# Dense blocks on chip for both halves of batch 0, a clock model with two levels, and weight loads on GpSimd's queue

## The chip, the cores and the metric

One core of a Trainium2 chip runs the whole program. The metric is the device time of one execution in microseconds; the time before is the median of three executions, 964.66 us. The engines are named TensorE (PE, with its weight loads as PEld), VectorE (DVE), ScalarE (ACT), GpSimd (POOL) and SyncE (SP), which issues DMAs.

## What is computed

The reference takes q, k and v of 4 batches, 8 heads, 576 positions and 64 dimensions. For each head it adds two attentions, then runs two feed-forward layers over the 2304 tokens (512 wide, 2048 inside):

```python
out_d = sm_attn(q_d, k_d, v_d)               # q, k, v averaged over groups of 4 positions
out_up = np.repeat(out_d, 4, axis=2)
mask = np.abs(pos[:, None] - pos[None, :]) < 4
attn = softmax(where(mask, scale * q @ k.T, -1e9))
x = (out_up + attn @ v)                      # -> [2304, 512]
x = prelu(x @ w_in1, alpha) @ w_out1
y = elu(x @ w_in2) @ w_out2
```

The weights come as 64-bit floats, so each must be converted on the chip.

## The kernel before, in words

The program is one function, `fused_kernel`, in which a planner writes out one order of instructions for all engines. Work is cut into generators ("threads": `th_...`), each with a priority; `_Clock` models when each engine, the SP queue and the DMA rings would be free, and `run_while`, `fill` and `tick` pick the next thread by priority among those whose inputs would be ready. Each engine then runs its instructions strictly in that written order. All instructions go through `_Engine.call` (line 231), so nearly every row of the profile has L231 and groups are told apart by tiles.

**Feed-forward.** Layer 1 has 8 token groups of 288 (two per batch: u = 0 and u = 1), each with 16 steps f of 128 inner columns. A step s multiplies x with `wi` (12 matmuls, tiles xh and xl, `mm_in`), applies the activation (`th_elem`: tiles n, r, gh, gl) and multiplies with `wo` (12 matmuls, `out1`). The list `segs` orders them: segment 0 is group 0 with f = 0 to 9, then group 1 with all 16, then the rest of group 0, then groups 2 to 7. Group 1 is u = 1 of batch 0; groups 2 and 3 are batch 1. Layer 2 has 6 groups of 384 tokens.

**Weights.** An item is one f of `w_in` or `w_out`, 512 KB of 64-bit words. `th_ldw` issues the loads (`load_w`: SP, tiles rawi and rawo), in the order of `items`. `th_conv` converts an item: ScalarE makes cp, VectorE does one instruction on cp and two into cw, ScalarE writes the high half of wi or wo and VectorE the low half (`raw_a` to `raw_d`). The raw item and the converted one share a slot. In layer 1 some slots hold attention tiles first (`early`), so `th_ldw` waits: items 8 to 15 for the local attention of u = 0 (`pav`), 16 to 19 for the sums of v, 24 to 31 for q and k. From the fifth item on (`PF = 4`) a load also waits until the item four before it has been converted that far. All these waits are on SP, whose queue runs in order: what is behind a waiting DMA waits too.

**Attention of batch 0.** `th_pair` and `th_da0` make the averaged attention (tiles sm, P, pt, od). The local attention of u = 0 is `th_dense`: blocks of 64 queries by 70 keys per pair of heads p = 0 to 3, with a mask added by a matmul (`d_mm`), maximum (`d_max`, tile Dmx), exponent (`d_exp`, tile dP), normalisation (`d_norm`, Dden), five transposes (`d_tp`, `d_ev`) and the product with v (`d_av`, tile vd), all on chip; then `p_add` makes x. When all four pairs are done, SP writes x to DRAM (xsp), to be read again for the third segment. The local attention of u = 1 goes another way: `th_S0` multiplies blocks of 72 by 78, evicts them (ss) and writes them to DRAM (scr); `th_soft0` reads only the band of 7 diagonals (tile s), takes the softmax and writes the band into a zeroed pscr; `th_p` reads dense blocks back (pp), transposes them (ppT), multiplies with vb and adds. Batch 1 does this for both halves; batches 2 and 3 use VectorE. Threads of u = 1 start after step 0 (`slot` 0).

**Clock and warm-up.** `_Clock.pe` books TensorE's columns by stretches of time and takes matmuls at full or half speed by what the stretch before held. In `run_while`, while step 0 is not ready and the planner sees TensorE idle, it inserts matmuls of a constant tile (warm) as long as `quiet()` holds: booked columns below `MORE * BUSY`.

Of the kernel before, what the change touches and what calls it, by code (L numbers as in the profile page):

```python
# [40 lines left out]
MORE = 1.0  # L41
# [12 lines left out]
NB = 2  # L54
# [3 lines left out]
class _Clock:  # L58
    TICK, BUSY = 10240 / 3, 2640.0
# [4 lines left out]
    MANY = {"ACT": 70.0, "DVE": 93.0, "SP": 50.0, "PE": 0.0}  # L64

    def __init__(self):
        self.cols = {}
        self.t = dict.fromkeys(("PE", "ACT", "DVE", "SP", "DMA"), 0.0)
# [11 lines left out]
    def pe(self, t, cost, share):  # L80
        k = int(t / self.TICK)
        while cost > 0.0:
            slow = 1.0 if self.cols.get(k - 1, 0.0) >= self.BUSY else 2.0
# [82 lines left out]
    def dma(self, out, in_):  # L166
# [21 lines left out]
class _Engine:  # L188
# [31 lines left out]
    def __getattr__(self, op):  # L220
        fn = getattr(self.eng, op)

        def call(*args, **kw):
            if op == "dma_start":
                self.clock.dma(kw["out"], kw["in_"])
# [10 lines left out]
def fused_kernel(ctx: ExitStack, tc: tile.TileContext, qk, vt, vl, ql, kl, vb, w_in1, w_out1, alpha,  # L236
# [3 lines left out]
    PE, ACT, DVE, SP = (_Engine(n, e, ck) for n, e in  # L240
                        (("PE", nc.tensor), ("ACT", nc.scalar), ("DVE", nc.vector), ("SP", nc.sync)))
# [12 lines left out]
    maskf = const.tile([128, 2, QK], F32, name="maskf")  # L254
    maskb = const.tile([128, 5, QK], BF16, name="maskb")
    identb = const.tile([128, 128], BF16, name="identb")
    warm = const.tile([128, 4], BF16, name="warm")

# [9 lines left out]
    scr0 = {(b, u): dram.tile([1, BLK * (RW + 1)], F32, name=f"scr{b}_{u}") for b in range(NB) for u in range(2) if b or u}  # L268
# [97 lines left out]
    def d_mm(p, bk):  # L366
        t = st["qk", 0, p]
        ps = bk[:, 0:5 * QK]
        mk = maskb.rearrange("p j k -> p (j k)")
# [9 lines left out]
    def d_max(p, bk):  # L379
        st["dP", p] = early(PT0 + p, [128, 5 * QK + 5 * 128], F32, f"dP_{p}")  # L380
        mx = Ap.tile([128, 5, 1], F32, tag="Dmx", name="Dmx", bufs=2)
        st["dmx", p] = mx
# [4 lines left out]
    def d_exp(p, bk):  # L387
        den = Ap.tile([128, 5, 1], F32, tag="Dden", name="Dden", bufs=2)
        st["dden", p] = den
        for j in range(5):  # L390
            c = slice(j * QK, (j + 1) * QK)
            ACT.activation(out=st["dP", p][:, c], in_=bk[:, c], func=AF.Exp, scale=float(D) ** -0.5,
                           bias=st["dmx", p][:, j], accum_out=den[:, j])

    def d_norm(p):
        den = st.pop(("dden", p))
        P = st["dP", p][:, 0:5 * QK].rearrange("p (j k) -> p j k", j=5)
# [4 lines left out]
    def d_tp(p, bks):  # L402
        for j in range(5):
            bk = bks[j // 4]
            PE.transpose(bk[0:QK, (j % 4) * 128:(j % 4 + 1) * 128], st["dP", p][:, j * QK:(j + 1) * QK], ident)

    def d_ev(p, bks):
        t = st["dP", p][0:QK, 5 * QK:]
# [3 lines left out]
    def d_av(p, bk):  # L412
        t, v = st.pop(("dP", p))[0:QK, 5 * QK:].rearrange("k (j c) -> k j c", j=5), st.pop(("vd", p))
# [447 lines left out]
    def th_S0(p, u):  # L861
        tag = "ss"
        yield "key", "ld0", p, u
        yield "tok", tag
        bks = yield "bank", 2
        s_mm(0, p, 4 * u, 4, bks)
        finish("smm", 0, p, u)
        yield ("ACT",)
        t = s_ev(4, bks, tag)
        release(bks)  # L870
        yield ("SP",)
        s_write0(0, p, u, t)
        put(tag)
        finish("S", 0, p, u)

# [11 lines left out]
    def th_dense(p):  # L887
        yield "key", "ld0", p, 0
        bks = yield "bank", 1
        d_mm(p, bks[0])  # L890
        finish("smm", 0, p, 0)
        finish("S", 0, p, 0)
        yield ("DVE",)
        d_max(p, bks[0])
        yield ("ACT",)
        d_exp(p, bks[0])
        release(bks)
        yield ("DVE",)
        d_norm(p)
        bks = yield "bank", 2  # L900
        d_tp(p, bks)
        yield ("ACT",)
        d_ev(p, bks)
        release(bks)
        yield "key", "od1", 0, p, (0,)
        bks = yield "bank", 1
        d_av(p, bks[0])
        finish("pav", 0, p, 0)
        yield ("DVE",)
        p_add(0, p, 0, bks[0])  # L910
        release(bks)
        x = st["x", 0, 0].rearrange("p k t j -> p k (t j)")
        yield ("ACT",)
        ACT.activation(out=xs["h"][:, p], in_=x[:, p], func=AF.Copy)
        yield ("DVE",)
        DVE.tensor_tensor(out=xs["l"][:, p], in0=x[:, p], in1=xs["h"][:, p].bitcast(F32), op=ALU.subtract)
        tm["x"] = max(tm["x"], ck.cur["t"])
        finish("xcp", p)
        finish("pa", 0, p, 0)
        if all(("pa", 0, z, 0) in done for z in range(NP)):  # L920
            finish("xa", 0, 0)
            SP.dma_start(out=xsp, in_=st.pop(("x", 0, 0)).rearrange("p k t j -> p k (t j)"))
# [132 lines left out]
    def th_soft0(b, u):  # L1055
        for p in range(NP):
            yield "key", "S", b, p, u
        if b and u:
            for p in range(NP):
                yield "key", "pr", b - 1, p, u  # L1060
# [39 lines left out]
    def th_vb(b, u):  # L1100
        if b:
            yield "key", "vb", b - 1 + u, 1 - u
# [123 lines left out]
    def th_ldw(ly):  # L1226
        for k, it in enumerate(items):
            if ly == 2:
                yield "key", "fr", (2,) + it
            else:  # L1230
# [4 lines left out]
                elif V0 <= k < SH0:  # L1235
                    yield "key", "sv", 0, k - V0
# [4 lines left out]
                if k >= PF:  # L1241
                    yield "key", "cv", 1, k - PF
# [189 lines left out]
    with tc.manual_schedule():  # L1432
# [3 lines left out]
        for p in range(NP):  # L1436
# [9 lines left out]
            if p:  # L1446
                at(0.0)
                load_vd(p - 1)
        at(0.0)
        load_vd(NP - 1)  # L1450
        at(0.0)
        ACT.activation(out=maskb[:, 0], in_=maskf[:, 0], func=AF.Copy)
        ACT.activation(out=maskb[:, 1:5], in_=maskf[:, 1:2].to_broadcast([128, 4, QK]), func=AF.Copy)
# [4 lines left out]
        for p in range(NP):  # L1458
# [110 lines left out]
def _prepare(np, a):  # L1569
# [39 lines left out]
    vd = np.stack([vp[0, :, o:o + QK] for o in QO], axis=1).reshape(NP, 2, 5, QK, D).transpose(0, 3, 2, 1, 4)  # L1609
    vd = vd.reshape(NP, QK, 5, 128)  # L1610
    md = np.full((128, 2, QK), -1e9, np.float32)
# [3 lines left out]
    md[:, 1][near] = 0.0  # L1615
    arrs = [qk, vt, vl, chunks(q, 0), chunks(k, HALO), vb, win(a["moe_w_in"]), wout(a["moe_w_out"]),
# [29 lines left out]
```

## Time and profile before

| | us |
|---|---|
| three executions | 962.89, 964.66, 969.34 |
| median | 964.66 |
| profiled execution | 970.52 |
| its span, first to last instruction | 968.7 |
| mean granted clock of TensorE, share of full | 0.974 |

The page's busy times overlap, since engines work beside each other; a share near 100% in a stage marks the candidate for what bounds it. PE's busy time holds time at half clock too, so it is read with the granted clock beside it. DMA waits are put down to the transfer that came last.

### The profile page before, as it was taken

To read this page: it belongs to the slowest core of one execution; us is meant where nothing else is said; L and a number is where in the kernel's file an instruction comes from. 1 tells how busy PE (TensorE), PEld (TensorE's weight loads), DVE (VectorE), ACT (ScalarE), POOL (GpSimd) and SP (SyncE) were. 2 spreads that over 40 slices of the span, in tenths; PEclk is the share of its full clock that TensorE was granted. 3 is DMA by queue.
4 is the path that set the end of the run, shared out by engine and by line. 5 is a ranking of instruction groups with operands and counts; after the bars stand their busy time and mean duration, and the time that the engine had idled before them with its cause. 6 is when DMAs were issued, how large, how long until landed. Compare 5 with 4: busy or idle time off the path is not lost.

```text
span 968.7 us, 16336 instructions
## 1 busy us (share of the span) xinstructions
PE 938.5 (97%) x6428; PEld 866.0 (89%) x6428; DVE 599.5 (62%) x1253; ACT 471.3 (49%) x1200; POOL 0.2 (0%) x4
## 2 busy tenths in 40 slices
PE   5978999899999999999999999999999999999998
PEld 3767889799999899999999999989999999998997
DVE  5778998645959789899638999732322322322222
ACT  5575678555432572332326677644443433433433
POOL 0000000000000000000000000000000000000000
PEclk9687999989999999999999999999999999999999
DMA  9277762534111523100207950003100100000000
GB/s 291 93 247 228 240 222 52 102 110 160 50 31 54 167 70 90 33 19 37 82 1 238 377 195 33 1 1 98 55 12 1 66 1 1 33 1 1 33 1 32
DMA packets 60933, 86.17 MB, mean 89 GB/s; under 512 B 29279, under 2 KB 40415, under 8 KB 60599
## 3 DMA queue, kind: packets, MB, share of 16 engines
q1 hardware_dynamic: 60857, 85.14, 28.0%
q8 instruction: 50, 0.82, 0.4%
q14 instruction: 26, 0.21, 0.1%
HBM read 69.93 MB, written 16.63 MB: 89 GB/s over the span
## 4 chain that ended last, share of the span: by engine, by line
PE 89%; DMA 6%; ACT 2%; DVE 2%; issue 1%; SPq 1%; ACTq 0%
PE bank L231 89%; DMA scr<-ss 2%; DMA s<-scr 1%; DMA qk<-in_qk_dram 1%; DMA pp<-pscr 1%; DMA pscr<-a 1%; SPq L231 1%; ACT dP L231 0%; DVE cw L231 0%; ACT ss L231 0%; ACT cp L231 0%; ACT P L231 0%; DVE s L231 0%; ACT n L231 0%; DVE cp L231 0%
## 5 line engine op out<-in xcount | busy, mean ns | idle before, releaser
L231 PE MATMUL bank<-xh,wi 128*128 128x288 f32 x1024 | 240.6, 304 | 3.6 <-DVE wi L231 2.8
L231 ACT ACTIVATE n<-bank 128x288 f32<-128x288 f32 (+1 forms) x224 | 99.4, 444 | 290.7 <-PE bank L231 290.5
L231 PE MATMUL bank<-gh,wo 128*128 128x288 f32 x1024 | 237.1, 302 | 1.2 <-ACT ys L231 1.2
L231 PE MATMUL bank<-x2h,wi 128*128 128x384 f32 x768 | 211.2, 337 | 0.0
L231 PEld LDWEIGHTS bank<-xh,wi 128*128 128x128 f32 x1024 | 176.4, 191 | 8.6 <-DVE wi L231 3.9
L231 PEld LDWEIGHTS bank<-gh,wo 128*128 128x128 f32 x1024 | 174.4, 190 | 6.3 <-issue 2.9
L231 PE MATMUL bank<-wo,gh 128*128 128x512 f32 x576 | 179.0, 392 | 0.0
L231 DVE SCALAR_TENSOR_TENSOR r<-n,bank 128x384 f32<-128x384 f32 x96 | 53.1, 554 | 195.0 <-ACT n L231 194.9
L231 ACT ACTIVATE gh<-r 128x288 fp32r<-128x288 f32 (+1 forms) x224 | 106.8, 477 | 100.2 <-DVE r L231 99.7
L231 PE MATMUL bank<-xl,wi 128*128 128x288 f32 x512 | 152.9, 299 | 0.0
L231 PE MATMUL bank<-gl,wo 128*128 128x288 f32 x512 | 151.8, 297 | 0.0
L231 DVE TENSOR_TENSOR gl<-r,gh 128x288 fp32r<-128x288 f32 (+1 forms) x224 | 111.4, 498 | 60.8 <-ACT gh L231 59.2
L231 PEld LDWEIGHTS bank<-x2h,wi 128*128 128x128 f32 x768 | 140.3, 188 | 3.9
L231 PE MATMUL bank<-x2l,wi 128*128 128x384 f32 x384 | 128.9, 336 | 0.0
L231 PEld LDWEIGHTS bank<-wo,gh 128*128 128x128 f32 x576 | 106.8, 188 | 18.2
L231 PE MATMUL bank<-wo,gl 128*128 128x512 f32 x288 | 113.8, 395 | 0.0
L231 DVE SCALAR_TENSOR_TENSOR r<-n,nal,bank 128x288 f32<-128x288 f32 x128 | 65.2, 509 | 53.1 <-ACT n L231 52.5
L231 PEld LDWEIGHTS bank<-xl,wi 128*128 128x128 f32 x512 | 98.0, 191 | 0.0
L231 PEld LDWEIGHTS bank<-gl,wo 128*128 128x128 f32 x512 | 97.3, 190 | 0.0
L231 PEld LDWEIGHTS bank<-x2l,wi 128*128 128x128 f32 x384 | 72.1, 188 | 3.8
L231 PEld LDWEIGHTS bank<-wo,gl 128*128 128x128 f32 x288 | 54.0, 187 | 11.5
L231 ACT ACTIVATE n<-n 128x384 f32<-128x384 f32 x96 | 50.4, 525 | 3.1
(101 smaller groups left out, 895.6 us busy)
## 6 DMA issues: line engine op xcount, KB each, us to landing
rawi<-in_w_in_dram SPq DMA_DIRECT2D x32, 512.0 KB
rawo<-in_w_out_dram SPq DMA_DIRECT2D x32, 512.0 KB
qk<-in_qk_dram SPq DMA_DIRECT2D x12, 582.0 KB
yT<-ys SPq DMA_DIRECT2D x32, 144.0 KB
out_dram<-os SPq DMA_DIRECT2D x18, 256.0 KB
vl<-in_vl_dram SPq DMA_DIRECT2D x4, 960.0 KB
vv<-in_vt_dram SPq DMA_DIRECT2D x12, 288.0 KB
kls<-in_kl_dram SPq DMA_DIRECT2D x12, 288.0 KB
```

Of the source, the lines that this page charges most:

```text
L231: return fn(*args, **kw)
```

## The change

- u = 1 of batch 0 takes the dense way as well: `th_dense(p, u)` with its own vd (four more loads of 70 x 640 floats on SP, ahead of the first step), a third mask, and its tiles dP and vd in the slots of items 16 to 23. `th_S0` goes; `th_soft0` and `th_p` serve batch 1 alone; `th_vb(1, 0)` no longer waits for batch 0. The conversion into xh and xl and the write of xsp stay with u = 0.
- All weight loads, of both layers, are issued by GpSimd instead of SP. The pacing by converted items (`PF`) goes. Before item 0, GpSimd copies one column of the last v tile, so it waits for that load. Items 8 to 15 wait as before, 16 to 23 now for u = 1's product with v.
- The clock model keeps a state: the first stretches count as full speed; from full speed the old level keeps it, from half speed a higher level is needed to rise. `quiet()` uses the level of the state. `dma` books an issue on GpSimd with 1000 ns.

```diff
@@ class _Clock
+    def fast(self, k):
+        while len(self.gear) <= k:
+            n = len(self.gear)
+            need = self.BUSY if n and self.gear[-1] else self.RISE
+            self.gear.append(n < self.FREE or self.cols.get(n - 1, 0.0) >= need)
+        return self.gear[k]
+
     def quiet(self):
         k = int(self.t["PE"] / self.TICK)
-        return self.cols.get(k, 0.0) < MORE * self.BUSY
+        return self.cols.get(k, 0.0) < (self.BUSY if self.fast(k) else self.RISE)
...
-        self.t["SP"] = max(self.t["SP"], self.deps("SP", outs, ins))
-        self.hw = max(self.hw + 25, self.t["SP"]) + 450
-        end = max(self.t["DMA"], self.hw + 650) + cost
+        self.t[eng] = max(self.t[eng], self.deps(eng, outs, ins))
+        if eng == "SP":
+            self.hw = max(self.hw + 25, self.t["SP"]) + 450
+            end = max(self.t["DMA"], self.hw + 650) + cost
+        else:
+            self.t[eng] += 1000
+            end = max(self.t["DMA"], self.t[eng] + 650) + cost
@@ load_w
-            SP.dma_start(out=raw[key], in_=wsrc[ly, nm][f])
+            GP.dma_start(out=raw[key], in_=wsrc[ly, nm][f])
...
-    def load_vd(p):
-        st["vd", p] = early(PP0 + p, [128, 5, 128], F32, f"vd_{p}")[0:QK]
-        SP.dma_start(out=st["vd", p], in_=vd[p])
+    def load_vd(p, u):
+        st["vd", p, u] = early((SH0 if u else PP0) + p, [128, 5, 128], F32, f"vd_{p}{u}")[0:QK]
+        SP.dma_start(out=st["vd", p, u], in_=vd[u, p])
@@ d_mm
         for j, o in enumerate(QO):
+            o += u * G1
...
-    def th_dense(p):
+    def th_dense(p, u):
         yield "key", "ld0", p, 0
+        if u:
+            yield "key", "sv", 0, p
...
-        yield "key", "od1", 0, p, (0,)
+        yield "key", "od1", 0, p, (u,)
+        if u:
+            yield "key", "xc", 0, 0
...
@@ th_ldw
-                elif V0 <= k < SH0:
-                    yield "key", "sv", 0, k - V0
+                elif V0 <= k < QK0:
+                    yield "key", "pav", 0, (k - V0) % NP, 1
...
-                if k >= PF:
-                    yield "key", "cv", 1, k - PF
+                if not k:
+                    yield "key", "ldv", NP - 1
+                    nc.gpsimd.tensor_copy(out=pace, in_=st["vv", 0, NP - 1][:, 0:1])
@@ spawning, batch 0
-            spawn(th_dense(p), -9 + p / 10)
-            spawn(th_S0(p, 1), US + p / 10, 0)
-            spawn(th_p(0, p, 1), UP + p / 10, 0)
-        spawn(th_soft0(0, 1), -10, 0)
-        spawn(th_vb(0, 1), UV, 0)
+            spawn(th_dense(p, 0), -9 + p / 10)
+            spawn(th_dense(p, 1), US + p / 10, 0)
```

## Rows read from the trace of the kernel before

**Rows 1.** The page, part 1 (engines) and part 4 (the chain by line)

```profile
PE 938.5 (97%) x6428; PEld 866.0 (89%) x6428; DVE 599.5 (62%) x1253; ACT 471.3 (49%) x1200; POOL 0.2 (0%) x4
PE bank L231 89%; DMA scr<-ss 2%; DMA s<-scr 1%; DMA qk<-in_qk_dram 1%; DMA pp<-pscr 1%; DMA pscr<-a 1%; SPq L231 1%; ACT dP L231 0%; DVE cw L231 0%; ACT ss L231 0%; ACT cp L231 0%; ACT P L231 0%; DVE s L231 0%; ACT n L231 0%; DVE cp L231 0%
```

**Rows 2.** Busy time of each engine by stage, from first converted load to layer 2

```profile
core 0: us, PE busy (x) PEld busy (x) DVE busy (x) ACT busy (x) POOL busy (x), PEclk, DMA share, GB/s
24.50:48.00 23.50, 22.78 (x210) 16.96 (x206) 17.97 (x42) 12.95 (x42) 0.00 (x0) 0.63 0.27 92
48.00:90.00 42.00, 33.24 (x257) 27.62 (x253) 31.57 (x72) 27.94 (x83) 0.00 (x0) 0.76 0.77 234
90.00:119.00 29.00, 27.93 (x271) 26.23 (x270) 27.90 (x55) 19.94 (x45) 0.00 (x0) 1.00 0.71 241
119.00:160.00 41.00, 39.85 (x346) 37.01 (x345) 38.78 (x77) 30.66 (x88) 0.00 (x0) 1.00 0.46 150
160.00:194.00 34.00, 29.76 (x267) 26.76 (x267) 21.43 (x52) 21.29 (x73) 0.00 (x0) 0.97 0.54 106
194.00:600.00 406.00, 405.33 (x3118) 391.42 (x3117) 322.71 (x690) 191.72 (x506) 0.00 (x0) 0.99 0.33 104
```

**Rows 3.** VectorE's conversion groups, 0 to 120 us: busy, mean ns

```profile
L231 DVE TENSOR_SCALAR cp<-cp 128x512 uint32<-128x512 uint32 x23 | 9.6, 419 | 0.0
L231 DVE SCALAR_TENSOR_TENSOR cw<-rawi,cp 128x512 uint32<-128x512 uint32 x12 | 8.3, 692 | 0.4
L231 DVE SCALAR_TENSOR_TENSOR cw<-rawi,cw 128x512 uint32<-128x512 uint32 x12 | 8.2, 686 | 0.1
L231 DVE SCALAR_TENSOR_TENSOR wi<-cw,wi 128x512 fp32r<-128x512 f32 x11 | 7.6, 688 | 4.7 <-ACT wi L231 4.6
```

**Rows 4.** Stretches of low granted clock

```profile
21.70:42.20 20.50, 20.11 (x177) 14.62 (x175) 15.49 (x41) 10.54 (x40) 0.00 (x0) 0.51 0.17 63
192.40:199.20 6.80, 5.39 (x28) 5.26 (x30) 1.83 (x5) 3.88 (x13) 0.00 (x0) 0.52 0.59 184
```

**Rows 5.** What TensorE waited for, 119 to 200 us

```profile
PE bank L231 <- DMA pp<-pscr: 4.2, 3, 2.3
```

**Rows 6.** What VectorE waited for, 20 to 120 us: total, times, longest

```profile
DVE wi L231 <- ACT wi L231: 4.6, 4, 1.9
DVE x L231 <- PE bank L231: 4.0, 6, 1.1
DVE s L231 <- DMA s<-scr: 2.3, 1, 2.3
```

**Rows 7.** The timeline of the SP queue: start us, us, issue

```profile
15.55 0.33 SPq L231 DMA_DIRECT2D rawi<-in_w_in_dram  x1
40.06 0.33 SPq L231 DMA_DIRECT2D xsp<-x  x1
46.48 0.36 SPq L231 DMA_DIRECT2D rawo<-in_w_out_dram  x1
```

**Rows 8.** 0 to 119 us: Dmx (DVE, ACT), Dden (DVE), s (DVE, ACT), dP (all), ppT

```profile
0.00:119.00 119.00, 2.77 (x8) 6.44 (x40) 0.83 0.69 219
0.00:119.00 119.00, 3.52 (x12) 0.83 0.69 219
0.00:119.00 119.00, 1.92 (x5) 0.39 (x1) 0.83 0.69 219
0.00:119.00 119.00, 7.81 (x100) 6.74 (x100) 2.10 (x4) 9.11 (x48) 0.83 0.69 219
0.00:119.00 119.00, 3.17 (x64) 2.66 (x64) 3.02 (x8) 0.83 0.69 219
```

**Rows 9.** 0 to 119 us, warm-up matmuls alone, tile warm (PE, PEld, DVE)

```profile
0.00:119.00 119.00, 12.66 (x60) 6.89 (x60) 0.06 (x1) 0.83 0.69 219
```

**Rows 10.** Instructions on tile cp alone, by stage (DVE, ACT)

```profile
24.50:48.00 23.50, 4.45 (x8) 3.20 (x5) 0.63 0.27 92
48.00:90.00 42.00, 11.09 (x20) 6.15 (x10) 0.76 0.77 234
```

More of the change, by code (lines that the diff above doesn't have):

```diff
@@ L63 @@
            ("DMA", "DVE"): 907.0, ("DMA", "PE"): 1003.0, ("ACT", "ACT"): 140.0}
-    MANY = {"ACT": 70.0, "DVE": 93.0, "SP": 50.0, "PE": 0.0}
+    MANY = {"ACT": 70.0, "DVE": 93.0, "SP": 50.0, "PE": 0.0, "GP": 50.0}
     def __init__(self):
-        self.cols = {}
-        self.t = dict.fromkeys(("PE", "ACT", "DVE", "SP", "DMA"), 0.0)
+        self.cols, self.gear = {}, []
+        self.t = dict.fromkeys(("PE", "ACT", "DVE", "SP", "DMA", "GP"), 0.0)
         self.t["SP"] = 560.0
@@ L82, in pe @@
         while cost > 0.0:
-            slow = 1.0 if self.cols.get(k - 1, 0.0) >= self.BUSY else 2.0
+            slow = 1.0 if self.fast(k) else 2.0
             part = min(cost, ((k + 1) * self.TICK - t) / slow)
@@ L164, in run, with dma @@
         return n * (8 if ap.dtype == U64 else 4)
-    def dma(self, out, in_):
+    def dma(self, out, in_, eng="SP"):
         outs, ins = [self.span(out)], [self.span(in_)]
@@ L224, in call @@
             if op == "dma_start":
-                self.clock.dma(kw["out"], kw["in_"])
+                self.clock.dma(kw["out"], kw["in_"], self.name)
             else:
@@ L239, in fused_kernel @@
     ck = _Clock()
-    PE, ACT, DVE, SP = (_Engine(n, e, ck) for n, e in
-                        (("PE", nc.tensor), ("ACT", nc.scalar), ("DVE", nc.vector), ("SP", nc.sync)))
+    PE, ACT, DVE, SP, GP = (_Engine(n, e, ck) for n, e in
+                            (("PE", nc.tensor), ("ACT", nc.scalar), ("DVE", nc.vector), ("SP", nc.sync),
+                             ("GP", nc.gpsimd)))
     const = ctx.enter_context(tc.tile_pool(name="const", bufs=1))
@@ L253, in fused_kernel @@
     nal = const.tile([128, NF], F32, name="nal")
-    maskf = const.tile([128, 2, QK], F32, name="maskf")
-    maskb = const.tile([128, 5, QK], BF16, name="maskb")
+    maskf = const.tile([128, 3, QK], F32, name="maskf")
+    maskb = const.tile([128, 2, 5, QK], BF16, name="maskb")
     identb = const.tile([128, 128], BF16, name="identb")
     warm = const.tile([128, 4], BF16, name="warm")
+    pace = const.tile([128, 1], F32, name="pace")
     W = {}
@@ L267, in fused_kernel @@
            for b in range(NB, B) for r in range(2) if r not in SDVE[b]}
-    scr0 = {(b, u): dram.tile([1, BLK * (RW + 1)], F32, name=f"scr{b}_{u}") for b in range(NB) for u in range(2) if b or u}
+    scr0 = {(b, u): dram.tile([1, BLK * (RW + 1)], F32, name=f"scr{b}_{u}") for b in range(1, NB) for u in range(2)}
     pscr = [dram.tile([1, BLK * (RW + 1)], F32, name=f"pscr{u}") for u in range(2)]
@@ L385, in d_max, with d_exp, d_norm @@
         DVE.tensor_scalar(out=mx, in0=mx, scalar1=-float(D) ** -0.5, scalar2=None, op0=ALU.mult)
-    def d_exp(p, bk):
+    def d_exp(p, u, bk):
         den = Ap.tile([128, 5, 1], F32, tag="Dden", name="Dden", bufs=2)
-        st["dden", p] = den
+        st["dden", p, u] = den
         for j in range(5):
             c = slice(j * QK, (j + 1) * QK)
[L392 to L397, printed above, removed]
+            ACT.activation(out=st["dP", p, u][:, c], in_=bk[:, c], func=AF.Exp, scale=float(D) ** -0.5,
+                           bias=st["dmx", p, u][:, j], accum_out=den[:, j])
+    def d_norm(p, u):
+        den = st.pop(("dden", p, u))
+        P = st["dP", p, u][:, 0:5 * QK].rearrange("p (j k) -> p j k", j=5)
         DVE.tensor_scalar(out=den, in0=den, scalar1=1e-9, scalar2=None, op0=ALU.add)
@@ L909, in th_dense @@
+        finish("pav", 0, p, u)
         yield ("DVE",)
-        p_add(0, p, 0, bks[0])
+        p_add(0, p, u, bks[0])
         release(bks)
[L912 to L922, printed above, removed]
+        if not u:
+            x = st["x", 0, 0].rearrange("p k t j -> p k (t j)")
+            yield ("ACT",)
+            ACT.activation(out=xs["h"][:, p], in_=x[:, p], func=AF.Copy)
+            yield ("DVE",)
+            DVE.tensor_tensor(out=xs["l"][:, p], in0=x[:, p], in1=xs["h"][:, p].bitcast(F32), op=ALU.subtract)
+            tm["x"] = max(tm["x"], ck.cur["t"])
+            finish("xcp", p)
@@ L924, in th_S @@
+        finish("pa", 0, p, u)
+        if all(("pa", 0, z, u) in done for z in range(NP)):
+            finish("xa", 0, u)
+            if not u:
+                SP.dma_start(out=xsp, in_=st.pop(("x", 0, 0)).rearrange("p k t j -> p k (t j)"))
     def th_S(b, p):
@@ L1057, in th_soft0 @@
             yield "key", "S", b, p, u
-        if b and u:
-            for p in range(NP):
-                yield "key", "pr", b - 1, p, u
         yield "tok", "s"
@@ L1447, in fused_kernel @@
                 at(0.0)
-                load_vd(p - 1)
+                load_vd(p - 1, 0)
         at(0.0)
-        load_vd(NP - 1)
+        load_vd(NP - 1, 0)
+        for p in range(NP):
+            at(0.0)
+            load_vd(p, 1)
         at(0.0)
-        ACT.activation(out=maskb[:, 0], in_=maskf[:, 0], func=AF.Copy)
-        ACT.activation(out=maskb[:, 1:5], in_=maskf[:, 1:2].to_broadcast([128, 4, QK]), func=AF.Copy)
+        ACT.activation(out=maskb[:, 0, 0], in_=maskf[:, 0], func=AF.Copy)
+        ACT.activation(out=maskb[:, 0, 1:5], in_=maskf[:, 1:2].to_broadcast([128, 4, QK]), func=AF.Copy)
+        ACT.activation(out=maskb[:, 1, 0:4], in_=maskf[:, 1:2].to_broadcast([128, 4, QK]), func=AF.Copy)
+        ACT.activation(out=maskb[:, 1, 4], in_=maskf[:, 2], func=AF.Copy)
         at(0.0)
@@ L1608, in _prepare @@
     zero = np.zeros((BLK, RW + 1), np.float32)
-    vd = np.stack([vp[0, :, o:o + QK] for o in QO], axis=1).reshape(NP, 2, 5, QK, D).transpose(0, 3, 2, 1, 4)
-    vd = vd.reshape(NP, QK, 5, 128)
-    md = np.full((128, 2, QK), -1e9, np.float32)
+    vd = np.stack([vp[0, :, u * G1 + o:u * G1 + o + QK] for u in range(2) for o in QO], axis=1)
+    vd = vd.reshape(NP, 2, 2, 5, QK, D).transpose(2, 0, 4, 3, 1, 5).reshape(2, NP, QK, 5, 128)
+    md = np.full((128, 3, QK), -1e9, np.float32)
     r, c = np.arange(128)[:, None] % QB, np.arange(QK)[None]
@@ L1615, in _prepare @@
     md[:, 1][near] = 0.0
+    md[:, 2][near & (c < QK - HALO)] = 0.0
     arrs = [qk, vt, vl, chunks(q, 0), chunks(k, HALO), vb, win(a["moe_w_in"]), wout(a["moe_w_out"]),
```

62 lines of the change are left out of this document (23 added, 39 removed).

## The prediction

> **What bounds the kernel now.** The page's engine list comes first [rows 1]: TensorE is busy for 938.5 of 968.7 us, so all its idle time together is 30.2 us. The chain by line says where to look: 89% is TensorE, and nearly all of the rest are DMAs of the tiles scr, s, pp and pscr, the way through DRAM that the local attention of batches 0 and 1 takes. Next come the windows by stage [rows 2]. From 194 to 600 us TensorE is busy for 405.33 of 406 us at a granted clock of 0.99. Nothing can be won there, and whatever the change adds on other engines lies under it. What can be won lies ahead of 194 us.
>
> In that head the bound changes twice. From 24.5 to 119 us, where the first segment (group 0, f = 0 to 9) runs, VectorE is busy for 17.97 + 31.57 + 27.90 = 77.44 of 94.5 us, and in the last 29 us of it for 27.90: it converts weights. One item costs it 0.419 + 0.692 + 0.686 + 0.688 = 2.49 us [rows 3]. A step of layer 1 needs two items, so VectorE gives out a step about every 5 us and TensorE waits for it in one form or another. TensorE's 100% and the half clock (20.11 of 20.5 us busy at 0.51 [rows 4]) therefore mislead in this stage: most of that slow work lies beside VectorE's. From 119 to 160 us both are full (39.85 and 38.78 of 41). From 160 to 194 us TensorE sits idle for 34 - 29.76 = 4.2 us, all of it for pp read back from pscr [rows 5], and after that the clock is low for 6.8 us [rows 4].
>
> So the currency of the first stage is VectorE's idle time: 94.5 - 77.4 = 17.1 us. Part has names [rows 6]: 4.6 for ScalarE's half of a conversion, 4.0 for TensorE, 2.3 for the scores' way through DRAM. The SP timeline gives the background [rows 7]: the fifth weight load is issued at 15.55, then the queue stands at the write of xsp until 40.06, and the sixth load goes out at 46.48.
>
> **Part 1, dense second half of batch 0.** It takes away, for u = 1 of batch 0, the scores through scr, one softmax, the way through pscr and the transposes of pp. It adds for each of four pairs what u = 0 does today. On VectorE the four pairs of u = 0 cost 2.77 (Dmx) + 3.52 (Dden and the product) = 6.3 us; the softmax gives back 1.92 and two short instructions on den, together about 2.4 us [rows 8]. Net +3.9 us on the engine that bounds the stage. On ScalarE it adds at most the 9.11 us of tile dP and takes away 3.02 (ppT) and four pairs of score evictions [rows 8]; ScalarE is busy for 12.95 + 27.94 + 19.94 = 60.8 of 94.5 us there, so this hides; without that cover it would cost some 5 us. On TensorE 7.81 us of transposes and products come for 3.17 plus the pp transposes; it hides in 10.5 us of idle time and in 12.66 us of warm-up matmuls [rows 2, 8, 9]. The four loads of vd for u = 1 (70 x 640 x 4 bytes each, 0.72 MB, 3.0 us at 241 GB/s [rows 2]) lie on SP behind everything that u = 0 needs and are wanted only after step 0: nothing. The wait of VectorE for s (2.3 us) goes; late next is x of u = 1, wanted at the second segment, some 60 us after step 0: no wait.
>
> **Part 2, weight loads on GpSimd.** SP loses 64 issues, which here take 0.33 to 0.36 us and up [rows 7], and with them all loads' places behind xsp, scr and pscr. POOL has 0.2 us of work today [rows 1], so nothing else is queued there but the four constants. The added wait, a copy that needs the last v load, holds only the weight loads behind it. In order behind one another now stand all 64; items 16 to 23 wait until u = 1 has been multiplied with its vd, about 15 to 20 us after step 0, which is done some 2 us after the write of xsp at 40.06 [rows 7], so near 60. VectorE reaches item 14 at 90 us today (28 instructions on cp, two an item [rows 10]); even if it gained 15 us it would want item 16 near 80, and 16 items of 512 KB take 35 us at 241 GB/s, the first of them 2. Loads arrive ahead of need. What that returns: VectorE's idle time in 24.5 to 90 us is 5.5 + 10.4 = 15.9 of the 17.1 us; from 90 us on, with items in stock, it is 1.1 of 29. With stock from the start I let 6 us stay: the 4.0 for TensorE, because step 0 still depends on the same u = 0 chain, and 2 for order. That returns 11.1 us. Bounds: 0 (the idle time lies in the written-out order, not in the loads) to 15.
>
> What a GpSimd DMA issue costs is in no row. By the nearest, an SP issue of 0.36 us [rows 7], the 32 of layer 1 cost between 0 (on an engine that has nothing else to do) and 11.5 us, if VectorE stood still for each. I take 0, since an SP issue holds up no other engine here, and keep 11.5 for the range. In layer 2 the same 32 loads lie beside 405.33 of 406 us of TensorE, with VectorE at 322.7: nothing, or if that cover were gone the same 11.5.
>
> The trace shows the loads standing behind xsp for 24.5 us [rows 7]. The Trainium skill, DMA: Bandwidth & Descriptors, Issuing engines are not separate DMA queues, says that issuing from several engines saves only the sequencer's issue time, since all run on the same 16 DMA engines. By that rule part 2 returns nothing but issues on SP, and what is left is case (a) below at its upper end. Row and rule differ in kind: what is saved is a place in a queue that waits, not bandwidth.
>
> **Part 3, two levels in the clock model.** The planner puts in more warm-up matmuls while it believes the clock low, and none where it believes it high. In the first stage that is worth at most VectorE's 4.0 us for TensorE, which I left in; it can cost as much if a filler delays the u = 0 chain. I take 0, range -4 to +4.
>
> **After the first segment.** From 119 us on TensorE is the bound, so the second segment starts earlier by what the first gains, if VectorE keeps up: it had 60.2 us of work in 75 [rows 2], and nothing is added there. At its end lie the waits for pp (4.2 us) and 6.8 us at half clock, 3.4 lost, 7.6 together. Batch 1 still goes through DRAM, but with no weight loads in SP's queue. I take half, 3.8; bounds 0 and 7.6.
>
> **The sum.** +3.9 - 11.1 - 3.8 = -11.0 us. The profiled execution took 970.52 us (span 968.7 and 1.8 around it), 5.9 above the median of three timings, 964.66, and 1.2 above the slowest. The difference goes to the median: 953.7 us.
>
> **Rivals.** (a) Nothing to speak of: the order written by hand puts conversions behind attention work, so VectorE's gaps stay or move to ScalarE; 0 to 7 us of idle time come back, 3.9 go to part 1, and the waits for pp stay. For it: 4.6 us of VectorE's waits are for ScalarE, not for a load [rows 6]. Against: they lie in the starved stretch. With the middle of it, 3.5 us, the time is 965 us (961.6 to 968.6).
> (b) Larger gain: in the stage up to 119 us only 2 us of idle time stay and the 7.6 us go whole: 3.9 - 15.1 - 7.6 = -18.8, 946 us. For it: from 90 to 119 us VectorE lost only 1.1. Against: u = 1's 6.3 us come ahead of conversions in priority.
> (c) Slower: GpSimd's issuing holds VectorE, or VectorE holds it. The place is VectorE between 20 and 130 us, where all 32 loads of layer 1 fall. The gain of 11.0 is gone at 0.34 us a load, and above 0.64 us a load (20.6 in all) the kernel is slower by over 1%. At one conversion instruction, 0.69 us [rows 3], it is 22: +11, 976 us. For it: VectorE is full there and POOL has never worked beside it in this trace. Against: the trace has no case at all.
> The Trainium skill speaks for (c): SBUF — State Buffer, SBUF: two separate sides, says that while VectorE runs an instruction in a two-port mode, GpSimd cannot write the descriptors of its DMAs, and that the one that comes second is blocked wholly. No run here shows it yet.
>
> **How the numbers follow.** About 1%, 9.6 us, is what a measurement of this kernel can tell from no change; faster by over 1% means below 955.0. The forecast gets 0.43; its own range is 947 to 960, the bounds above taken half way, so of it 0.30 is faster and 0.13 the same. (a) gets 0.25, nearly all the same: 0.24. (b) 0.20, all faster. (c) 0.12, slower, with 0.01 of (a): 0.13. Faster 0.50, same 0.37, slower 0.13. The range runs from 938, where (b) also takes the 4 us of part 3 and some of the half clock before, to 970, the middle between no change and (c).
>
> **What would show it.** Right: weight loads on a queue of their own, the next after the fifth well before 46 us; VectorE's idle time from 24.5 us to the end of segment 1 near 6 us; the end of the first segment some 7 us before 119; 0 us of waits for scr and s ahead of 120 us; from 200 us on the same busy shares. Wrong: VectorE's conversions longer than 0.42 and 0.69 us, or gaps beside POOL's issues (c); the same idle time with the raw weights long landed (a); a segment 3 that starts at 194 us although segment 1 ended earlier (batch 1's way through DRAM sets it).

## The result: 1.1% slower, and the profile after

The changed kernel takes 975.41 us (median of four, 973.75 to 976.37); the kernel before took 963.78 in four executions of that comparison. The ratio is 1.011, with a 95% interval from 1.0087 to 1.0133: about 1.1% slower, outside the predicted range of 938 to 970. The profiled execution took 975.99 us, with a span of 974.1.

The page of the changed kernel, parts 1, 4 and 6, answers to [rows 1]. The last two lines give KB a load and the median us from issue to landing.

```profile
PE 933.7 (96%) x6424; PEld 860.7 (88%) x6424; DVE 600.9 (62%) x1266; ACT 474.8 (49%) x1233; POOL 34.6 (4%) x69
...
PE 82%; DMA 7%; DVE 5%; ACT 4%; issue 1%; SPq 0%; POOL 0%; ACTq 0%; DVEq 0%
...
rawi<-in_w_in_dram POOLq DMA_DIRECT2D x32, 512.0 KB, 6.6
rawo<-in_w_out_dram POOLq DMA_DIRECT2D x32, 512.0 KB, 6.0
```

TensorE's idle time grew from 30.2 us (968.7 less 938.5) to 40.4, and that with 7.2 us less of warm-up matmuls (5.51 against 12.66 [rows 9]). By the medians a weight load lands 6.6 or 6.0 us after its issue.

The windows of the changed kernel by stage, as in [rows 2]:

```profile
24.50:48.00 23.50, 18.20 (x179) 13.75 (x180) 14.94 (x38) 11.42 (x40) 4.76 (x9) 0.64 0.84 289
48.00:90.00 42.00, 33.91 (x287) 27.44 (x286) 38.40 (x90) 31.40 (x111) 1.05 (x2) 0.84 0.42 157
90.00:119.00 29.00, 25.61 (x243) 23.50 (x244) 28.31 (x57) 21.26 (x55) 7.57 (x14) 1.00 0.66 252
119.00:160.00 41.00, 36.86 (x304) 34.08 (x304) 32.96 (x66) 26.92 (x78) 0.00 (x0) 0.92 0.29 97
160.00:194.00 34.00, 30.07 (x278) 27.52 (x275) 23.18 (x56) 19.74 (x64) 0.00 (x0) 1.00 0.45 93
194.00:600.00 406.00, 403.37 (x3127) 388.86 (x3126) 319.09 (x687) 192.64 (x515) 17.08 (x32) 1.00 0.33 105
```

Between 48 and 90 us VectorE does 38.40 us of work against 31.57, a part of it the dense blocks' own. But at the start it does 14.94 where it did 17.97, and from 119 to 160 us 32.96 where it did 38.78, while TensorE loses 3 us (36.86 against 39.85) where it had been full. The timeline of GpSimd's queue shows the loads (start, duration, idle time before):

```profile
18.32 0.18 POOL L1244 COPY pace<-v 128x1 f32<-128x1 f32 x1 [17.88 <-DMA v<-in_vt_dram]
18.44 0.66 POOL L241 DMA_DIRECT2D rawi<-in_w_in_dram  x1
...
21.69 0.53 POOL L241 DMA_DIRECT2D rawi<-in_w_in_dram  x1
28.50 0.54 POOL L241 DMA_DIRECT2D rawo<-in_w_out_dram  x1 [6.29 <-issue]
...
82.03 0.53 POOL L241 DMA_DIRECT2D rawi<-in_w_in_dram  x1 [36.16 <-DVE x L241]
...
99.23 0.53 POOL L241 DMA_DIRECT2D rawi<-in_w_in_dram  x1 [13.98 <-PE bank L241]
```

They come in bursts. Seven go out by 22 us, but ScalarE starts on the first only at 28.2. Items 16 and 17 go out at 82 and 85 us, and the other fourteen between 99 and 113. ScalarE's timeline, first and third item:

```profile
28.21 0.66 ACT L241 ACTIVATE cp<-rawi 128x512 f32<-128x512 f32 x1 [3.58 <-DMA rawi<-in_w_in_dram]
...
40.23 0.67 ACT L241 ACTIVATE cp<-rawi 128x512 f32<-128x512 f32 x1
```

The third load left at 19.61, yet its conversion starts at 40.23, with no wait for a DMA. In the kernel before, that load left at 14.14 and its conversion started at 37.40. Of the waits of TensorE and ScalarE from 20 to 130 us, these hang on loads and other transfers (total, times, longest):

```profile
PE bank L241 <- ACT pt L241: 4.8, 1, 4.8
...
PE bank L241 <- ACT ys L241: 4.1, 1, 4.1
...
ACT cp L241 <- DMA rawi<-in_w_in_dram: 3.9, 2, 3.6
ACT ys L241 <- DMA yT0a<-ys: 3.8, 1, 3.8
```

These are two chains. ScalarE stands in its written order at the first conversion, whose load has not landed, and pt behind it keeps TensorE for 4.8 us. The second is at the end of the first segment, when the partial sum of group 0 is evicted (ys) and written to DRAM (yT0a). This write is issued at 118.8 us, while loads are landing, and takes 6.05 us; ScalarE waits for it 3.8 us, TensorE 4.1.

### The profile page after: what moved, and what is told of

It reads as the page before. It is cut to its first block, busy times and chain, and to the rows that moved or that the text cites. A ratio compares the mean times of both kernels' runs of the same rounds, so it can differ in the third digit from the quotient of the medians.

```text
span 974.1 us, 16413 instructions
## 1 busy us (share of the span) xinstructions
PE 933.7 (96%) x6424; PEld 860.7 (88%) x6424; DVE 600.9 (62%) x1266; ACT 474.8 (49%) x1233; POOL 34.6 (4%) x69
## 4 chain that ended last, share of the span: by engine, by line
PE 82%; DMA 7%; DVE 5%; ACT 4%; issue 1%; SPq 0%; POOL 0%; ACTq 0%; DVEq 0%
PE bank L241 82%; DMA qk<-in_qk_dram 2%; DVE cw L241 2%; DMA yT<-ys 1%; DMA v<-in_vt_dram 1%; DMA rawo<-in_w_out_dram 1%; ACT P L241 1%; DMA yT0a<-ys 1%; DMA pscr<-a 1%; ACT cp L241 1%; DVE r L241 0%; ACT n L241 0%; ACT ys L241 0%; SPq L241 0%; DVE cp L241 0%
## 5 line engine op out<-in xcount | busy, mean ns | idle before, releaser
L241 PE MATMUL bank<-xh,wi 128*128 128x288 f32 x1024 | 243.4, 306 | 7.1 <-ACT wi L241 4.1
L241 ACT ACTIVATE gh<-r 128x288 fp32r<-128x288 f32 (+1 forms) x224 | 106.9, 477 | 112.0 <-DVE r L241 111.5
```

## The experiments

Three theories at first. Q: the queue change makes the loss. D: the dense blocks do, as VectorE work. W: the clock model does, through other warm-up matmuls. Later ones, named in the expectations, are P (the plan's landing time), B (bursts), H (held slots) and L (a lucky order). Ratios are to the kernel before in the same comparison.

### Which of the three parts

Two edits, alone and together, give the other six combinations. The first puts the loads back on SP, the second takes the two-level clock model out:

```diff
-            GP.dma_start(out=raw[key], in_=wsrc[ly, nm][f])
+            SP.dma_start(out=raw[key], in_=wsrc[ly, nm][f])
...
-                if not k:
-                    yield "key", "ldv", NP - 1
-                    nc.gpsimd.tensor_copy(out=pace, in_=st["vv", 0, NP - 1][:, 0:1])
+                if k >= PF:
+                    yield "key", "cv", 1, k - PF
```

```diff
-            slow = 1.0 if self.fast(k) else 2.0
+            slow = 1.0 if self.cols.get(k - 1, 0.0) >= self.BUSY else 2.0
...
-        return self.cols.get(k, 0.0) < (self.BUSY if self.fast(k) else self.RISE)
+        return self.cols.get(k, 0.0) < self.BUSY
```

On the changed kernel the first gives dense_clock, the second dense_gp, both dense_only. The inverse of the second on the kernel before gives clock_only, that of the first gp_only, both clock_gp.

clock_only: 

> Only the two-level clock model; attention of u = 1 and weight loads as before. Theory Q (the loss comes from the weight loads on GpSimd's queue: late first load, held items 16 to 23, then a burst that the yT0a writes stand behind): within 3 us of 963.8, half-clock time ahead of 120 us a few us less or more. Theory D (the loss is the 3.9 us of VectorE work of the dense second half, and the order that follows from it): the same, within 3 us. Theory W (the warm-up fillers delay the chain to step 0): 967 to 970.

gp_only: 

> Only the weight loads on GpSimd, without pacing; u = 1 still through DRAM, clock model as before. Theory Q: slower, 968 to 976, with ScalarE waiting some 3 us for the first rawi near 25 us. Theory D: within 3 us of 963.8, or faster by up to 8, since the items come earlier and VectorE has no added work. Theory W: within 3 us of 963.8.

clock_gp: 

> Clock model and GpSimd loads, u = 1 through DRAM. Theory Q: as with GpSimd's loads alone, 968 to 976. Theory D: within 3 us of 963.8 or faster. Theory W: 967 to 970 if the fillers cost, whatever the loads do.

dense_only: 

> Only the dense second half; weight loads on SP with the old pacing, slots 16 to 23 held by its tiles until the product with vd, clock model as before. Theory Q: within 3 us of 963.8 or up to 5 faster (four transfers less on the way of u = 1). Theory D: 968 to 976, VectorE busy some 4 us more up to 119 us and the first segment later by as much. Theory W: within 3 us of 963.8.

dense_clock: 

> The changed kernel with its weight loads back on SP and paced by conversions as before; dense second half and clock model stay. Theory Q (GpSimd's queue makes the loss): back to 960 to 967. Theory D (the dense second half makes it): stays at 970 to 977.

dense_gp: 

> The changed kernel with the old clock model. Theory Q and theory D: 972 to 978, as the changed kernel, within 3 us. Theory W (the fillers cost): 966 to 970.

| parts in it | loads on SP | loads on GpSimd |
|---|---|---|
| neither | before | gp_only 976.25, 1.0107 [1.0077, 1.0137] |
| clock model | clock_only 961.68, 0.9953 [0.9936, 0.9970] | clock_gp 977.09, 1.0112 [1.0085, 1.0139] |
| dense blocks | dense_only 963.74, 0.9980 [0.9957, 1.0003] | dense_gp 975.08, 1.0086 [1.0054, 1.0118] |
| both | dense_clock 962.58, 0.9968 [0.9956, 0.9981] | changed 975.41, 1.0110 [1.0087, 1.0133] |

Theory Q holds: in every row the right column is 1.1 to 1.6 points above the left. (gp_only and clock_gp end 0.3 and 1.1 us above the range that Q gave them.) Without GpSimd's queue the other parts are worth 0.2 to 0.5%. D and W fall.

### Pacing and the number of loads in flight

pf_on_gp keeps the old pacing on GpSimd, no_pace takes out the copy that waits for v:

```diff
                     nc.gpsimd.tensor_copy(out=pace, in_=st["vv", 0, NP - 1][:, 0:1])
+                if k >= PF:
+                    yield "key", "cv", 1, k - PF
```

```diff
-                if not k:
-                    yield "key", "ldv", NP - 1
-                    nc.gpsimd.tensor_copy(out=pace, in_=st["vv", 0, NP - 1][:, 0:1])
```

pf_on_gp: 

> The changed kernel with the old pacing kept on GpSimd's queue (a load waits until the item four before it is converted), so that no burst of 16 loads goes out near 100 us. Theory Q: 966 to 971, the wait of ScalarE for yT0a (3.8 us) and of TensorE behind it (4.1 us) gone, the low clock after 124 us too. Theory D: within 2 us of 975.4.

no_pace: 

> The changed kernel without the copy that makes GpSimd wait for the last load of v, so weight loads begin at once and share the rings with q, k and v. Theory Q: the stall of ScalarE for the first rawi (3.6 us) goes but the loads of q and k land later by the share that eight loads of 512 KB take, up to 4.2 MB or 15 us; 975 to 985. Theory D: the same direction, 975 to 985; it does not tell the two apart but prices the wait that the change added.

They took 974.98 us (1.0104 [1.0070, 1.0139]) and 980.23 us (1.0142 [1.0106, 1.0179]). Neither mends it, and for pf_on_gp theory Q had forecast 966 to 971 us. There, thirteen of the last sixteen loads still leave between 106.9 and 119.4 us, and ScalarE waits 4.5 us for yT0a: the pacing holds in the plan alone, and GpSimd does not wait for the conversions. In no_pace the wait for the first load is down to 0.4 us, that for yT0a stays at 4.1. The next kernel limits the loads in flight on the chip:

```diff
             yield ("DMA",)
+            old = (ly,) + items[k - 2]
+            if ly == 1 and k >= 2 and old in raw:
+                nc.gpsimd.tensor_copy(out=pace, in_=raw[old].bitcast(F32)[:, 1:2])
             load_w((ly,) + it)
```

depth2: 

> The changed kernel with at most two layer-1 loads in flight on GpSimd's queue: before load k GpSimd copies one word of load k-2, and so waits for its landing. The written order of the other engines stays. Theory B expects 964 to 969 us, with yT0a landing in under 4 us after its issue (7.78 in the changed kernel) and the first load landing before 25 us (28.2). Theory P expects no gain, 974 to 980 us: each load lands as late as before or later against the same order. Theory H expects 974 to 980 us too.

It took 973.69 us, 1.0098 [1.0072, 1.0123]. What theory B forecast did not come. But the first load landed at 26.0 us and ScalarE still waited 3.0 us for yT0a (3.8 in the changed kernel), so fewer loads in flight did not make the transfers timely, and what timely ones would be worth stays untested. (The 7.78 us in the expectation is the length of a row of four issues with that wait among them; yT0a's landing took 6.05.) Its timeline of GpSimd times single loads, since the copy ahead of load k ends the wait for load k-2:

```profile
16.68 0.66 POOL L241 DMA_DIRECT2D rawi<-in_w_in_dram  x1
...
26.02 0.18 POOL L1248 COPY pace<-rawi 128x1 f32<-128x1 f32 x1 [8.15 <-DMA rawi<-in_w_in_dram]
...
30.79 0.53 POOL L241 DMA_DIRECT2D rawi<-in_w_in_dram  x1 [0.28 <-issue]
...
35.30 0.21 POOL L1248 COPY pace<-rawi 128x1 f32<-128x1 f32 x1 [1.60 <-DMA rawi<-in_w_in_dram]
...
41.16 0.53 POOL L241 DMA_DIRECT2D rawi<-in_w_in_dram  x1 [0.48 <-ACT xh L241]
...
52.24 0.18 POOL L1248 COPY pace<-rawi 128x1 f32<-128x1 f32 x1 [8.05 <-DMA rawi<-in_w_in_dram]
```

With SP quiet a load lands 4.5 us after its issue (30.79 to 35.30). The first, issued behind SP's loads of v, vd and vb, takes 9.3 (16.68 to 26.02), and the one issued at 41.16, just before SP's zero writes and its loads of qk and vv, takes 11.1. Two in flight are late as well.

### Which loads

```diff
-            GP.dma_start(out=raw[key], in_=wsrc[ly, nm][f])
+            eng = GP if ly == 1 and f < 8 else SP
+            eng.dma_start(out=raw[key], in_=wsrc[ly, nm][f])
```

gp_last16 has `f >= 8` there; both keep the copy and the old pacing.

gp_first16: 

> The changed kernel with only the first 16 layer-1 loads on GpSimd's queue, the other 16 and all of layer 2 on SP's, paced as in the kernel before. Theory H expects 961 to 965 us, no loss, since the held items are back on SP. If the late start (the first load issued only at 18.4 us and landing at 28.2) is what costs, 971 to 977 us. Theory P expects something between, 966 to 973 us, by the share of loads whose landing is misjudged.

gp_last16: 

> The changed kernel with the last 16 layer-1 loads on GpSimd's queue, the first 16 and all of layer 2 on SP's. Theory H expects the whole loss, 972 to 977 us. A late start as the cause expects 961 to 966 us, since the start is that of the kernel with the loads on SP. Theory P expects 966 to 973 us.

They took 965.66 us (1.0013 [0.9998, 1.0027]) and 967.64 us (1.0037 [1.0022, 1.0051]). Against dense_clock's 0.9968, the same kernel with all loads on SP, that is 0.45 and 0.69 points, 1.14 together, where all loads cost 1.42. Each half carries a share: neither the late start alone nor the held slots alone (H). (965.66 lies between the ranges of H and P.) And each half shows one of the two chains: gp_first16 has the wait for the first load (ScalarE 3.2 us, TensorE 4.5 for pt) and none for yT0a; gp_last16 has the wait for yT0a (ScalarE 4.1, TensorE 4.0) and only 0.7 us for rawi.

### What the planner believes of a load's landing

The planner keeps its own clock and writes the order of every engine by it. This edit tells it that GpSimd's loads land 5 us later than it reckons, and changes nothing else by hand:

```diff
         self.t["DMA"] = end
+        if eng == "GP":
+            end += 5000.0
         self.note("DMA", outs, ins, end)
```

late2 and late10 have 2000.0 and 10000.0. sp_late5 is dense_clock with the same lines for the weight loads on SP (`if in_.dtype == U64:`).

late5: 

> The changed kernel with one number altered in the planner: it is told that a weight load on GpSimd's queue lands 5 us later than it reckons. Queue, pacing and loads are as in the changed kernel; the written order of all engines is planned anew. Theory P (the plan is at fault: engines stand in a written order made for loads that land sooner than they do, and stall there) expects most of the 11 to 13 us back: 963 to 969 us, and PE's and ScalarE's waits for the first weights gone. Theory B (bursts: up to seven loads lie in flight on the second queue and make the small transfers of SP's queue, scr, s, yT0a, late) expects little, 971 to 978 us, because the bursts stay. Theory H (held slots: the loads of items 16 to 31 come too late, whatever the plan says) expects 972 to 978 us.

late2: 

> As late5 with 2 us in place of 5. Theory P (the planner takes GpSimd's loads to land earlier than they do; the plan's error is what costs) expects part of the loss back, since the median load lands 6.0 to 6.6 us after its issue: 963 to 973 us. Theory L (late5 was one lucky order; any new plan falls somewhere between 960 and 980 us) expects no relation to the 2 us.

late10: 

> As late5 with 10 us in place of 5. Theory P expects 961 to 967 us: no load is then planned before it lands, and the surplus costs only some idle time at the start. Theory L expects anything from 960 to 980 us.

sp_late5: 

> The run dense_clock (loads on SP's queue) with the planner told that the weight loads land 5 us later: a sham, since those loads land as the plan reckons. Theory P expects no gain, 961 to 967 us against dense_clock's 962.58. If slack in the plan helps whatever the queue, it would gain, 956 to 960 us. Theory L expects anything from 960 to 980 us.

| told, us later | on GpSimd | on SP |
|---|---|---|
| 0 | 975.41, 1.0110 [1.0087, 1.0133] | 962.58, 0.9968 [0.9956, 0.9981] |
| 2 | 967.91, 1.0042 [1.0024, 1.0060] | |
| 5 | 961.16, 0.9962 [0.9938, 0.9985] | 962.73, 0.9993 [0.9968, 1.0019] |
| 10 | 967.94, 1.0031 [1.0012, 1.0050] | |

One number in the plan gives back 14 us (1.8 us more than P's range allows) with queue, loads and copy as they were; on SP the same number gains nothing. 2 us give half. 10 us give no more than that, and end just above what P expected: from 90 to 119 us VectorE then has 21.35 us of work, where late5 has 27.59. The windows of late5:

```profile
24.50:48.00 23.50, 18.32 (x254) 13.91 (x253) 22.14 (x60) 18.42 (x77) 4.99 (x9) 1.00 1.01 404
48.00:90.00 42.00, 37.63 (x289) 31.20 (x288) 38.57 (x84) 31.79 (x92) 1.05 (x2) 0.84 0.25 88
90.00:119.00 29.00, 24.69 (x233) 21.42 (x232) 27.59 (x54) 20.30 (x54) 7.41 (x14) 0.88 0.90 336
119.00:160.00 41.00, 39.88 (x350) 37.20 (x349) 37.24 (x82) 32.07 (x98) 0.00 (x0) 1.00 0.31 66
160.00:194.00 34.00, 34.00 (x315) 32.16 (x315) 17.06 (x36) 17.63 (x53) 0.00 (x0) 1.00 0.32 87
```

VectorE works 22.14 us of the first 23.5 (14.94 in the changed kernel), TensorE's granted clock there is 1.00 (0.64), and from 119 to 194 us TensorE is idle for 1.1 us (8.1 in the changed kernel). The loads still come in bursts, as GpSimd's timeline and the page's part 6 of late5 show:

```profile
16.32 0.66 POOL L243 DMA_DIRECT2D rawi<-in_w_in_dram  x1
...
19.57 0.53 POOL L243 DMA_DIRECT2D rawi<-in_w_in_dram  x1
26.13 0.54 POOL L243 DMA_DIRECT2D rawo<-in_w_out_dram  x1 [6.04 <-DVE dmx L243]
...
71.32 0.53 POOL L243 DMA_DIRECT2D rawi<-in_w_in_dram  x1 [34.15 <-DVE x L243]
...
91.77 0.53 POOL L243 DMA_DIRECT2D rawi<-in_w_in_dram  x1 [15.99 <-DVE gl L243]
...
rawi<-in_w_in_dram POOLq DMA_DIRECT2D x32, 512.0 KB, 6.0
```

The loads land nearly as late as before, but no engine stands waiting for them: from 20 to 130 us the waits of late5 hold neither ScalarE's for rawi and yT0a nor those of TensorE's matmuls for pt and ys. So in the changed kernel the loss lies in the written order: another order, with the same loads on the same queue, gives it back.

That the order was bad because the plan takes loads to land too soon (P) is shown in part. With nothing ahead of it, the plan books 3.1 us for a load on GpSimd's queue (1000 ns of issue, 650, and 512 KB at 360 bytes a ns), where the medians are 6.6 and 6.0. In late5 the first conversion stands behind other work and waits no more, as P says. But three things don't fit P alone. First, loads on SP are late as well, against what the expectation of sp_late5 takes for granted. The plan books 2.6 us for one, and in dense_clock, where ScalarE has the same instructions ahead of it, the first was read 8.2 us after its issue (9.8 in the changed kernel):

```profile
16.69 0.35 SPq L241 DMA_DIRECT2D rawi<-in_w_in_dram  x1
...
24.92 0.67 ACT L241 ACTIVATE cp<-rawi 128x512 f32<-128x512 f32 x1 [0.61 <-DMA rawi<-in_w_in_dram]
```

Second, late2 gains its 7.5 us with the first chain still there:

```profile
ACT cp L243 <- DMA rawi<-in_w_in_dram: 3.6, 1, 3.6
...
PE bank L243 <- ACT pt L243: 5.8, 3, 4.0
```

What is gone in late2 is the wait for yT0a, and the edit doesn't touch the landing time that the plan has for yT0a (`self.t["DMA"]` is set above the added lines). In late5, too, the last load leaves 11.8 us ahead of yT0a's first write (108.4 and 120.2), in the changed kernel 6.2. Why the new orders avoid this wait was not tried. Third, theory L, that any new order falls between 960 and 980 us, holds all three results. Against it: the kernels with dense blocks and all loads on GpSimd took 973.7 to 980.2 us without the number, and 961.2 to 967.9 with it.

late5 also beats the kernel before, as clock_only and dense_clock do; their intervals overlap, and none of the three is shown to be the best.

### Without the dense blocks

If the plan's landing time were all, the same number would mend gp_only. gp_late5 is gp_only with it; gp_pf is gp_only with the old pacing kept in the plan, gp_late5_pf has both:

```diff
+        if eng == "GP":
+            end += 5000.0
```

```diff
                     nc.gpsimd.tensor_copy(out=pace, in_=st["vv", 0, NP - 1][:, 0:1])
+                if k >= PF:
+                    yield "key", "cv", 1, k - PF
```

gp_late5: 

> The kernel before with the loads on GpSimd's queue alone (the run gp_only) and the planner told that they land 5 us later. Theory P expects 962 to 968 us, 8 us or more below gp_only's 976.25. Theory L expects about 976 us as likely as not.

gp_pf: 

> gp_only with the pacing of the kernel before kept on GpSimd's queue (load k only after the conversion of item k-4), the plan's landing time unchanged. In gp_only and in gp_late5 the read of s from scr, issued at 64.1 and 64.3 us, landed only 10 us later, behind some 16 loads issued between 38 and 62 us. Theory B (there the cost is that burst) expects that wait of VectorE for s to fall from 10.1 us to 3 or less and 966 to 971 us. Theory P (the plan's landing time) expects 972 to 978 us, as for the changed kernel with that pacing (974.98).

gp_late5_pf: 

> gp_only with both: the pacing kept and the planner told that a GpSimd load lands 5 us later. If burst and plan both cost in this kernel, 961 to 967 us, and below gp_pf by 2 us or more. Theory B alone expects the time of gp_pf. If neither is the cause there, 973 to 978 us.

gp_late5 took 976.63 us, 1.0139 [1.0097, 1.0181]: not mended, against what P expected. ScalarE waits for no weight load in either kernel from 20 to 130 us, so there was no first chain to remove. Here the second half of batch 0 still goes through scr. SP's timeline and the waits of VectorE and TensorE (20 to 120 us) of gp_only:

```profile
64.08 0.31 SPq L235 DMA_DIRECT2D s<-scr  x1
...
DVE s L235 <- DMA s<-scr: 10.1, 1, 10.1
...
PE bank L235 <- ACT od L235: 9.7, 1, 9.7
```

and VectorE's same wait in gp_late5:

```profile
DVE s L237 <- DMA s<-scr: 10.0, 1, 10.0
```

In the kernel before that wait was 2.3 us [rows 6]. TensorE stands 9.7 us behind it in gp_only (for od, behind ScalarE's work on s), 9.5 in gp_late5. The read of s is issued at 64.1 us; seventeen loads left between 38.5 and 67.4 us, four of them at 61.7, 62.3, 66.3 and 66.9. By these traces SP's own small transfer comes late among the loads; a better landing time for the loads doesn't touch it.

Theory B expected the pacing to mend this. It did not: gp_pf took 987.58 us, 1.0247 [1.0207, 1.0287], and gp_late5_pf 980.63 us, 1.0173 [1.0140, 1.0206]. gp_pf lies above both ranges expected of it; gp_late5_pf lies above its two ranges and 7 us below gp_pf, whose time theory B alone expected of it. GpSimd's timeline and VectorE's waits (20 to 200 us) of gp_pf:

```profile
40.81 0.53 POOL L235 DMA_DIRECT2D rawo<-in_w_out_dram  x1 [4.08 <-PE bank L235]
41.43 0.53 POOL L235 DMA_DIRECT2D rawi<-in_w_in_dram  x1
...
DVE s L235 <- DMA s<-scr: 15.6, 2, 14.1
```

Eight loads still leave between 40.8 and 47.2 us, since the pacing is in the plan only, and the wait for s grew to 14.1 us. That the loads in flight make s late is read from these traces, not isolated: no kernel here spread the loads on the chip and kept the way through scr. Why the pacing costs another 11 us here stays open. The landing time gives 7 of them back (987.58 to 980.63), where P and B together had promised 961 to 967 us.

## Why the prediction was wrong

**Part 2, the loads on GpSimd: the step that failed.** It put -11.1 us on VectorE's idle time, with "Loads arrive ahead of need" and with 0 for GpSimd's issues. Issued earlier they were: the eighth load at 28.5 us, against 46.48 for the sixth before [rows 7]. But the first landed too late for its place in the order, and the third was not converted sooner for leaving early (40.23 us, 37.40 before). That is the sign that the prediction itself named for rival (a), idle time with the raw weights landed. VectorE's idle time from 24.5 to 119 us is 94.5 - 81.65 = 12.8 us, not 6, and its 4.2 us of added work are about what the dense blocks bring: next to nothing of the 11.1 came. In place of a gain the queue cost 13 us (975.41 against 962.58). The lower bound of 0 ("the idle time lies in the written-out order, not in the loads") was the right idea and not deep enough: the order is written anew for each kernel and can come out worse.

**The currency failed too.** In late5 VectorE's idle time is 94.5 - 88.3 = 6.2 us, close to the 6 that was forecast. With the loads on SP and the same number told (sp_late5) it is 94.5 - 88.19 = 6.3:

```profile
24.50:119.00 94.50, 79.61 (x764) 66.09 (x763) 88.19 (x194) 70.47 (x222) 0.00 (x0) 0.89 0.59 210
```

So the order gives this time back, not the queue. And it is not worth its length in the end: late5 took 961.16 us, 0.4% less than the kernel before, with 10.9 us of idle time gone. The first segment did not end sooner, by the first write of yT0a in the kernel before, the changed one and late5:

```profile
118.98 0.80 SPq L231 DMA_DIRECT2D yT0a<-ys  x2
...
118.82 7.78 SPq L241 DMA_DIRECT2D yT0a<-ys  x4
...
120.24 0.80 SPq L243 DMA_DIRECT2D yT0a<-ys  x2
```

In dense_clock, with 9.0 us of idle time, it ended at 113.7, some 5 us sooner, and the time was 962.58. What bounds the head of the kernel when VectorE's idle time is gone stays open.

The Trainium skill, DMA: Bandwidth & Descriptors, Issuing engines are not separate DMA queues, says that issuing from several engines saves issue time only. Late5 beside dense_clock (0.9962 and 0.9968) agrees: with that order the move is worth nothing that can be measured. That loads on a second queue may hold up SP's small transfers, as the traces of yT0a and s suggest, stood in no rival.

**Items 16 to 23** were put "near 60". They left at 82 us and later. In late5 two left at 71 and 75 us and the rest from 92 us on, and it is 14 us faster: wrong; whether the 7 to 11 us between the two kernels matter was not tried.

**Part 1, the dense half: right in size, wrong in effect.** From 0 to 119 us the tiles Dmx and Dden take 5.44 and 7.11 us of VectorE, 6.3 more than before [rows 8], as forecast, and the softmax on s is gone there. That this costs the end nearly 4 us was wrong: dense_only's ratio is 0.9980 with an interval up to 1.0003, so no cost is seen.

**Part 3, the clock model: the value was wrong, the range held.** Taken as 0 with -4 to +4; alone it gave 3.7 us by the medians (965.4 and 961.68). In clock_only TensorE works 33.41 of 34 us between 160 and 194, where it had 29.76 [rows 2].

**After the first segment.** A gain of 3.8 us was forecast. TensorE's idle time from 119 to 194 us rose from 5.4 us to 8.1. In late5 it fell to 1.1, 4.3 less than before: that size was right for an order that the forecast did not have.

**Rivals.** (c) gave 976, the time that came, but not by its mechanism. GpSimd's issues took 0.53 us each, near the 0.64 from which (c) was to decide, but VectorE stood still for none of them. VectorE's conversion groups of the changed kernel, 0 to 120 us, answer to [rows 3]:

```profile
L241 DVE TENSOR_SCALAR cp<-cp 128x512 uint32<-128x512 uint32 x24 | 10.1, 422 | 0.0
L241 DVE SCALAR_TENSOR_TENSOR cw<-rawi,cp 128x512 uint32<-128x512 uint32 x12 | 8.3, 692 | 0.4
L241 DVE SCALAR_TENSOR_TENSOR cw<-rawi,cw 128x512 uint32<-128x512 uint32 x12 | 8.2, 686 | 0.1
L241 DVE SCALAR_TENSOR_TENSOR wi<-cw,wi 128x512 fp32r<-128x512 f32 x11 | 7.5, 684 | 0.0
```

They are what they were (419, 692, 686 and 688 ns). The Trainium skill, SBUF — State Buffer, SBUF: two separate sides, named with (c), says that while VectorE runs an instruction in a two-port mode, GpSimd cannot write descriptors. No run here shows which of VectorE's instructions run in such a mode; what shows is no blocking. Of the seven issues from 99.9 to 103.5 us six take 0.53 us and one 0.71, with VectorE busy for 28.31 of 29 us around them. The prediction's own test, longer conversions, rejected (c) from the first trace, so its 976 us was met by luck. Rival (a), no gain worth the name, is what the queue is worth with the order of late5.

## What to carry to other kernels

Where a program writes the order of its engines from a cost model, moving a transfer to another queue also writes a new order, and the two are judged together: 975 and 961 us here with the same queue. So measure issue to landing in the first trace, for both queues, give the model that time, and try more than one value; if the time jumps with the value, it is the order that is being measured. A pacing that exists only in the plan paces nothing on a queue of its own. Idle time on the busiest engine of a stage is worth its length only if the end of the stage moves with it: look for the instruction that ends the stage. And before loads are let run ahead, list the small transfers that others wait for and that will land among them.

## What was not expected of the hardware

A 512 KB load with at most one other in flight landed after 4.5 us with SP quiet, and after 9.3 to 11.1 us beside SP's large transfers (depth2). On SP's queue it is alike: in dense_clock the load issued at 18.57 us landed after 7.60, the one at 96.22 after 3.84. In these traces the landing time goes with what else is moving, more than with the queue or with how many loads GpSimd has out. After seven issues 0.53 us apart the eighth waited 6.29 us in the changed kernel, where the profile names no releaser ("issue"), but 0.75 in gp_only; what it waited for was not tried.
